# An attention, gated-MLP and RWKV kernel on one core: filler matmuls on TensorE during the first batch's attention

## The chip, the cores and the metric

The kernel runs on one core of one Trainium2 chip. The metric is the device time in microseconds (us) of one execution. Several executions are timed and their median is given; one further execution is taken by the hardware profiler, and all views of the trace come from that one.

## The reference

Three layers follow each other: attention with a causal window of 128 keys and a distance bias, a gated MLP with a matmul along the sequence, and an RWKV channel mix.

```python
def _attn_ref(q, k, v):                     # (4, 8, 576, 64)
    scores = scale * np.matmul(q, k.transpose(0, 1, 3, 2))
...
    scores = np.where(mask, scores + bias[None], -1000000000.0)
...
    return np.matmul(attn, v).astype(np.float32)

def _moe_ref(x, w_in, g_ln, w_sg, b_sg, w_out):      # x (4, 576, 512), w_in (512, 1024)
    h = x @ w_in
...
    u, v = (h[..., :d_ff // 2], h[..., d_ff // 2:])
...
    v_s = np.einsum('ts,bsd->btd', w_sg, v_n) + b_sg[None, :, None]
    gated = u * v_s
    return (x + gated @ w_out).astype(np.float32)

def _moe2_ref(x, mu_k, mu_r, w_k, w_v, w_r):
...
    k = np.maximum(xk @ w_k, 0.0)
    v = k * k @ w_v
    r = 1.0 / (1.0 + np.exp(-(xr @ w_r)))
    return (r * v).astype(np.float32)
```

## The kernel before, in words

**Tiles.** Sequences of 576 rows are cut into five tiles of at most 128. A product in float32 is done in most places as three float32r matmuls of a high and a low part; the first eight heads' scores and all products of attention weights and values are plain float32 matmuls.

**Stages.** The four batches have eight heads each. The loop `for n in range(9)` (line 1117) records the attention of the first batch, one `slot(n)` per head: scores into a bank of PSUM (`s_bank`, tile `s`), bias, row extreme and exponential (`s_tile`, tiles `p`, `nmax`, `sum`, `rin`), transposes of the weights (`t1_step`, `t2_step`, tile `t`, copied to `pf`), and for each pair of heads the product with the values (`av_step`, tile `a`, copied to `x`; a last piece of it goes into a score bank, so that `s<-pf,rawv` is part of it). Beside the heads, eight pieces of `w_in` (float64, taken apart on ScalarE and VectorE) become `w_in_t`. From the second batch on (line 1128), the attention of batch b + 1 is merged with the gated MLP of batch b (`moe1`, tiles `d`, `gt`, `u`, `v`, `gg`). The first gated-MLP matmul is `d<-w_in_t,xg`; it needs the attention output of all eight heads of the first batch. `phase2` is the channel mix over all rows.

**What sets the order.** All operations are recorded first (`Rec.op`), each with its engines and estimated costs in ns, and what it depends on. `Rec.rank` gives each a due time, for TensorE its place in the running sum `pe_time` of TensorE's costs. `Rec.schedule` then plays the engines in a list simulation: a free engine takes the ready operation with the earliest due time; an operation with several engines goes where the plan sees it end first. The sorted start times are the order in which the instructions are written, engine by engine. On the chip each engine runs its queue in that order.

**Buffers.** PSUM has three pools: `psD` (four buffers, tiles `d`, `a`, `wps`), `psS` (two banks, tile `s`), `psT` (two, tile `t`).

**Names that the change touches.** `wps` (line 1093) is a tile of `psD` that takes the results of ten matmuls of zeros at the start, which nobody reads. `K.tri` is a constant bfloat16 tile of ones and zeros in two triangles, written by GpSimd at the start. `Build.mm` (line 368) records a group of matmuls as one operation; the matmuls themselves all have line 377, transposes line 385.

Of the kernel before, what the change touches and what calls it, by code (L numbers as in the profile page):

```python
# [9 lines left out]
F32 = mybir.dt.float32  # L10
# [10 lines left out]
P = 128  # L21
# [109 lines left out]
class Rec:  # L131
# [6 lines left out]
        "pool": {"pe": 92.0, "act": 64.0, "dve": 64.0, "pool": 120.0, "sp": 100.0},  # L138
        "sp": {"pe": 0.0, "act": 0.0, "dve": 0.0, "pool": 0.0, "sp": 0.0},
    }  # L140
    BIAS_DP, BIAS_DA, BIAS_AP = 3000.0, 1500.0, 1500.0

    def __init__(self):
        self.ops, self.tags, self.psum = [], {}, set()
        self.bufs = {}
        self.after = {}
        self.open_pool = None
        self.pe_time = 0.0

# [93 lines left out]
    def schedule(self):  # L243
        ops = self.ops
        engs = ("pe", "act", "dve", "pool", "sp")
        free = {e: 0.0 for e in engs}
        q = {e: [] for e in engs}
        soon = []
        for o in ops:
            o.indeg, o.start = len(o.deps), None  # L250
            o.rdy = {a[0]: 0.0 for a in o.alts}
            if not o.indeg:
                for a in o.alts:
                    heapq.heappush(soon, (0.0, o.i, a[0]))
        t = 0.0
        done = 0
        dma_free = 0.0
        held = {"dve": 0.0, "pool": 0.0}
        other = {"dve": "pool", "pool": "dve"}

        def begin(o, e, t):
            return max(t, held[other[e]]) if o.port[e] else t
        wake = []
        while done < len(ops):
            while soon and soon[0][0] <= t:
                _, i, e = heapq.heappop(soon)
                o = ops[i]
                if o.start is not None:
                    continue
                bias = 0.0  # L270
                if len(o.alts) > 1:
                    names = [a[0] for a in o.alts]
                    if e == "dve":
                        bias = self.BIAS_DP if "pool" in names else self.BIAS_DA
                    elif e == "act" and "pool" in names:
                        bias = self.BIAS_AP
                    bias += ENG.get((o.lab, "/".join(names), e), 0.0)
                heapq.heappush(q[e], (o.lst + bias, i))
            moved = False
            for e in engs:  # L280
                if free[e] > t:
                    continue
                h = q[e]
                while h and ops[h[0][1]].start is not None:
                    heapq.heappop(h)
                if not h:
                    continue
                if e == "sp" and dma_free > t + 2500.0:
                    soon_sp = dma_free - 2500.0
                    heapq.heappush(wake, soon_sp)  # L290
                    continue
                o = ops[heapq.heappop(h)[1]]
                a = next(x for x in o.alts if x[0] == e)
                if len(o.alts) > 1:
                    best = min(begin(o, x[0], max(free[x[0]], t, o.rdy[x[0]])) + x[1] for x in o.alts)
                    if begin(o, e, t) + a[1] > best + 1e-6 and begin(o, e, t) + a[1] > o.lst + 100.0:
                        heapq.heappush(h, (-1e18, o.i))
                        alt = None
                        sk = []
                        while h:  # L300
                            z = heapq.heappop(h)
                            oz = ops[z[1]]
                            if oz.start is not None:
                                continue
                            az = next(x for x in oz.alts if x[0] == e)
                            bz = min(begin(oz, x[0], max(free[x[0]], t, oz.rdy[x[0]])) + x[1] for x in oz.alts)
                            if begin(oz, e, t) + az[1] > bz + 1e-6 and begin(oz, e, t) + az[1] > oz.lst + 100.0:
                                sk.append(z)
                                continue
                            alt = oz  # L310
                            break
                        for z in sk:
                            heapq.heappush(h, z)
                        if alt is None:
                            continue
                        o = alt
                        a = next(x for x in o.alts if x[0] == e)
                o.start, o.eng = t, a
                if e == "sp":
                    free[e] = t + 475.0  # L320
                    dma_free = max(dma_free, t + 1125.0) + a[1]
                    o.end = dma_free + 1300.0
                else:
                    t0 = begin(o, e, t)
                    free[e] = t0 + a[1]
                    o.end = t0 + a[1]
                    if o.port[e]:
                        held[e] = t0 + a[1]
                done += 1
                moved = True  # L330
                for c in o.outs:
                    c.indeg -= 1
                    for x in c.rdy:
                        c.rdy[x] = max(c.rdy[x], o.end + self.LAT[e][x])
                    if not c.indeg:
                        for x in c.rdy:
                            heapq.heappush(soon, (max(c.rdy[x], t), c.i, x))
            if moved:
                continue
            nxt = [f for f in free.values() if f > t]  # L340
            if soon:
                nxt.append(max(soon[0][0], t))
            while wake and wake[0] <= t:
                heapq.heappop(wake)
            nxt += wake[:1]
            assert nxt
            t = min(nxt)
        self.makespan = max(o.end for o in ops)
        return sorted(ops, key=lambda o: (o.start, o.i))


class Build:
# [132 lines left out]
    def dma(self, out, in_, nbytes, reads=(), writes=(), nominal=None):  # L485
        nc = self.nc
        return self.r.op([("sp", nbytes / 330.0, lambda: nc.sync.dma_start(out=real(out), in_=real(in_)))],
                         [in_, *reads], [out, *writes], nominal=nominal)

    def raw(self, eng, cost, go, reads, writes):  # L490
        return self.r.op([(eng, cost, go)], reads, writes)
# [3 lines left out]
def attn_gmlp_rwkv_kernel(  # L495
# [19 lines left out]
    K = Build(nc)  # L515
# [7 lines left out]
    late = ("w2", "raw2")  # L523
# [3 lines left out]
    def T(pool, shape, dtype, tag, name=None, bufs=None):  # L527
        return R.tile(pool, shape, dtype, tag, name or tag, bufs)
# [41 lines left out]
    def cols(w, kk, half):  # L570
        k = w.shape[1] // 2
        return w[kk * P:(kk + 1) * P, half * k:(half + 1) * k]
# [24 lines left out]
    def load_head(n):  # L597
        if n >= NH:
            return
        b, h = divmod(n, H)  # L600
        pt = ("qk", "QK") if plain_s(n) and n in ODD else ("raw", "raw")
        rawqk[n] = T(pt[0], [P, 2, S], F32, pt[1], "rawqk")
        K.dma(rawqk[n], qkT[b, h], P * 2 * S * 4)
# [178 lines left out]
    def av_step(n):  # L782

        b, c = n // H, n % H // 2
        a = T("psD", [P, 4, P], F32, "d", "a")
        its, a4 = [], []
        p4 = PTc.pop((n, 1)) if fold(n) else None
        for r0, m in ((0, n), (64, n + 1)):
            rv = rawv.pop(m)
            ar = a[r0:r0 + 64]  # L790
            if fold(m):
                pf = PTc.pop((m, 0))
                its.append([(ar[:, ki:min(ki + 2, 4), :], rv[:, ki, :], pf[:, ki::4, :], ki == 0, ki == 3, SG) for ki in range(4)])
                k = m - n
# [16 lines left out]
                it.append((ar[:, 384:512], rv[:, 3, :], pf[:, 0, :], False, True, SG))  # L811
                its.append(it)
            a4.append((r0, rv, (pf[:, 1, 0:64], pf[:, 1, 64:128])))
        K.mm([x for y in zip(*its) for x in y])
        A4.append((n, a4))
        if c == 0:
            x_t[b] = T("xp", [P, NC, S + 1], F32, "x")
            z = x_t[b][:, :, 0:1]
# [2 lines left out]
        if n + 2 == NH:  # L821
            a4_step(T("psS", [P, 2, 256], F32, "s", "a4"))

    XG = {}

    def xsplit(b, c):
        if c == 0:
# [264 lines left out]
    K.raw("dve", 200, lambda: nc.vector.memset(real(wz), 0.0), [], [wz])  # L1092
    wps = T("psD", [P, 512], F32, "d", "wps")
    K.mm([(wps, wz[:, 0:128], wz, True, True, {})] * NWARM)
    load_head(0)
    K.raw("pool", 1100, lambda: nc.gpsimd.memset(real(K.tri), 1.0), [], [K.tri])
    for u in range(2):
# [17 lines left out]
    K.ts(mus1.flat(), mus.flat(), -1.0, 1.0, ALU.mult, ALU.add)  # L1115
    K.raw("dve", 60, lambda: nc.vector.memset(real(mhalf), -0.5), [], [mhalf])
    for n in range(9):
        for i, (_, f) in enumerate(slot(n)):
            f()
            if i == 3 and n + 2 < H:  # L1120
                mask_head(n + 2)
        for i in ((0, 1), (2, 3), (4,), (5,), (6,), (7,), (), (), ())[n]:
            kk, half = i % 4, 1 - i // 4
            c = slice(half * 512, half * 512 + 512)
            raw = None
            if wide:
                raw = (st0, st1)[i // 4][:, i % 4]
            job(w_in_t[:, kk, 0, c], w_in_t[:, kk, 1, c], cols(w_in, kk, half), 512, raw=raw, dec=("tp", "t"))
    for b in range(B):
        a = []  # L1130
        for n in range(8 * (b + 1) + 1, 8 * (b + 2) + 1):
# [2 lines left out]
        d = moe1(b)  # L1134
# [6 lines left out]
        if b == B - 1:  # L1141
# [3 lines left out]
            for i in range(8):  # L1145
                kk, half = i % 4, i // 4
                c = slice(half * 512, half * 512 + 512)
                k = 5 + i
# [81 lines left out]
```

## Time and profile before

| what | value |
|---|---|
| median of 3 runs | 617.51 us (616.62 to 618.85) |
| the profiled execution, own time | 618.84 us |
| its span, first to last instruction | 616.9 us |
| mean granted TensorE clock | 0.982 |
| TensorE matmuls, busy | 596.0 us, 97% of the span |
| VectorE, ScalarE, GpSimd, busy | 450.3, 343.9, 191.6 us |
| bytes moved | 57.74 MB |

The span is shorter than the execution's time by what lies ahead of the first and behind the last instruction, 1.9 us. The granted clock is the share of TensorE's full speed (2.4 GHz) that the chip allowed: 0.50 is 1.2 GHz, and a mean between the two levels says for what part of the time each held. A busy time is the time in which an engine had an instruction at work.

### The profile page before, as it was taken

The numbers are of one execution on the slowest core, as the hardware profiler recorded it, in microseconds if no ns is written. First come the engines' busy times: TensorE is split into PE (matmuls) and PEld (weight loads), VectorE is DVE, ScalarE is ACT, GpSimd is POOL, SyncE is SP. The second block draws the span as 40 slices with busy tenths as digits, with TensorE's granted clock in tenths as the row PEclk, the third lists the DMA queues.
The fourth block names the chain that finished last, engine by engine and source line by source line (L and its number), as shares of the span: only waits on it lengthen the run. The fifth ranks groups of instructions, "written<-read, shape, count | busy, mean of one in ns | idle before, by whom it ended". The sixth has DMA issues, their size and how long they took to land.

```text
span 616.9 us, 10182 instructions
## 1 busy us (share of the span) xinstructions
PE 596.0 (97%) x3538; PEld 505.0 (82%) x3538; DVE 450.3 (73%) x1204; ACT 343.9 (56%) x868; POOL 191.6 (31%) x334
## 2 busy tenths in 40 slices
PE   7777999999999999999999999999999999999997
PEld 4554879999789997889979998787888888888896
DVE  5777699999999999998588998894581349226122
ACT  5987889776887555875246547632531333234031
POOL 5455474335575457632234430001020001000000
PEclk9978899999999999999999999999999999999999
DMA  8954423323413134010171437413002000000100
GB/s 307 322 162 143 142 78 109 115 78 102 157 56 99 61 99 155 22 61 12 31 254 67 136 112 249 134 63 102 35 17 69 17 1 35 35 1 1 52 17 35
DMA packets 25331, 57.74 MB, mean 94 GB/s; under 512 B 4416, under 2 KB 13120, under 8 KB 24768
## 3 DMA queue, kind: packets, MB, share of 16 engines
q1 hardware_dynamic: 25280, 57.09, 28.0%
q8 instruction: 28, 0.46, 0.3%
q14 instruction: 23, 0.19, 0.1%
HBM read 47.63 MB, written 9.45 MB: 93 GB/s over the span
## 4 chain that ended last, share of the span: by engine, by line
PE 85%; DVE 8%; ACT 4%; issue 1%; DMA 1%; POOL 1%; SPq 0%; ACTq 0%; DVEq 0%; POOLq 0%
PE d L377 47%; PE vps L377 16%; PE s L377 7%; PE rps L377 6%; PE a L377 5%; PE t L385 3%; ACT p L399 1%; PE tf L385 1%; DVE p L680 1%; DVE wdec L455 1%; ACT pf L407 1%; DMA rawqk<-in_qk_dram 1%; DVE QK L419 1%; DVE gt L455 1%; ACT wdec L553 0%
## 5 line engine op out<-in xcount | busy, mean ns | idle before, releaser
L377 PE MATMUL d<-xk,wk 128*128 128x512 f32 (+1 forms) x480 | 105.3, 368 | 0.0
L377 PEld LDWEIGHTS d<-xk,wk 128*128 128x128 f32 x480 | 84.6, 188 | 16.2 <-ACT rl L399 0.2
L377 PE MATMUL vps<-w_v_t,k2h 128*128 128x512 f32 x288 | 94.8, 396 | 0.3 <-DVE w_v_t L409 0.3
L399 ACT ACTIVATE p<-p,nmax 128x256 f32<-128x256 f32 (+3 forms) x160 | 76.6, 480 | 28.5 <-DVE nmax L680 27.7
L680 DVE CUSTOM_DVE_ANT_0 p<-s,mask 128x256 f32<-128x256 f32 (+3 forms) x160 | 60.2, 383 | 12.8 <-PE s L377 12.2
L377 PE MATMUL d<-w_sg_t,vhl 128*128 128x288 f32 x448 | 66.5, 298 | 0.0
L399 ACT ACTIVATE rl<-d 128x512 f32<-128x512 f32 (+1 forms) x40 | 22.1, 554 | 78.3 <-PE d L377 75.0
L377 PEld LDWEIGHTS vps<-w_v_t,k2h 128*128 128x128 f32 x288 | 54.1, 188 | 13.8 <-DVE w_v_t L409 0.7
L377 PEld LDWEIGHTS d<-w_sg_t,vhl 128*128 128x128 f32 x448 | 60.9, 188 | 0.7 <-issue 0.2
L377 PE MATMUL d<-w_in_t,xg 128*128 128x512 f32 (+1 forms) x240 | 60.8, 398 | 0.0
L377 PE MATMUL d<-xg,w_in_t 128*128 128x288 f32 x384 | 57.0, 298 | 2.0 <-DVE u L455 2.0
L377 PE MATMUL vps<-w_v_t,k2l 128*128 128x512 f32 x144 | 57.0, 396 | 0.0
L377 PE MATMUL d<-gg,w_out_t 128*128 128x288 f32 x384 | 56.7, 298 | 0.0
L377 PEld LDWEIGHTS d<-xg,w_in_t 128*128 128x128 f32 x384 | 52.1, 188 | 3.1 <-DVE u L455 2.6
L377 PE MATMUL rps<-w_r_t,xr 128*128 128x512 f32 x216 | 54.4, 390 | 0.0
L377 PEld LDWEIGHTS d<-gg,w_out_t 128*128 128x128 f32 x384 | 52.0, 188 | 0.9 <-issue 0.3
L409 DVE CAST k2h<-rl 128x512 fp32r<-128x512 f32 (+1 forms) x28 | 10.9, 388 | 55.3 <-ACT rl L427 55.2
L377 PEld LDWEIGHTS d<-w_in_t,xg 128*128 128x128 f32 (+1 forms) x240 | 41.0, 177 | 10.9
L419 DVE TENSOR_TENSOR r<-vps,r 128x512 f32<-128x512 f32 x18 | 12.4, 691 | 48.7 <-PE vps L377 48.7
L377 PEld LDWEIGHTS rps<-w_r_t,xr 128*128 128x128 f32 x216 | 40.3, 188 | 8.4
L475 POOL TENSOR_SCALAR p<-p,rin 128x128 f32<-128x128 f32 (+4 forms) x63 | 35.3, 570 | 35.9 <-DVE rin L703 27.3
L482 ACT ACTIVATE p<-p,rin 128x128 f32<-128x128 f32 (+4 forms) x86 | 33.3, 429 | 8.3 <-DVE rin L703 8.2
(130 smaller groups left out, 1166.7 us busy)
## 6 DMA issues: line engine op xcount, KB each, us to landing
rawqk<-in_qk_dram SPq DMA_DIRECT2D x32, 576.0 KB, 3.9
rawv<-in_v_dram SPq DMA_DIRECT2D x32, 160.0 KB, 2.5
xs<-x SPq DMA_DIRECT2D x4, 1154.0 KB, 5.8
out_dram<-r SPq DMA_DIRECT2D x18, 256.0 KB, 2.0
st<-in_w_in_dram SPq DMA_DIRECT2D x8, 512.0 KB, 6.8
wraw<-in_w_k_dram SPq DMA_DIRECT2D x8, 512.0 KB, 3.8
wraw<-in_w_v_dram SPq DMA_DIRECT2D x8, 512.0 KB, 3.5
wraw<-in_w_out_dram SPq DMA_DIRECT2D x8, 256.0 KB, 3.3
```

Source lines behind the costliest of these rows:

```text
L377: pe.matmul(real(o), real(l), real(r), start=st, stop=sp, **ex)
L385: pe.transpose(real(o), real(i), real(d))
L399: nc.scalar.activation(real(out), real(in_), func, scale=scale, **kw)
L407: alts.append(("act", self._act(in_), lambda: nc.scalar.copy(real(out), real(in_))))
L409: alts.append(("dve", self._dve(in_.n, not in_.ps), lambda: nc.vector.tensor_copy(real(out), real(in_))))
L419: alts.append(("dve", self._dve(out.n, False), lambda: nc.vector.tensor_tensor(real(out), real(a), real(b), op)))
L455: alts.append(("dve", cost or self._dve(out.n, False, isinstance(s, Vw)), lambda: nc.vector.scalar_tensor_tensor(real(out), real(a), real( ...
L475: alts.append(("pool", 240 + out.n if ptr else 150 + 0.83 * out.n, lambda: nc.gpsimd.tensor_scalar(real(out), real(a), real(s1), real(s2), ...
L482: alts.append(("act", self._act(a, 1), lambda: nc.scalar.mul(real(out), real(a), real(s1))))
L680: K.raw("dve", 70 + w / 0.96, lambda: nc.vector.tensor_tensor_reduce(out=real(pw), in0=real(si), in1=real(ma), scale=-0.125, scalar=3.0e38 ...
```

## The change

`Build.filler` records a list of up to 220 single matmuls that are no operations of the plan: each multiplies a 128x128 block of `K.tri` with 256 columns of `K.tri` into `wps`, which nobody reads. The list opens with a matmul of the same shape that is an operation, and ends with another (`filler_end`), which depends on the attention output `AV[k]` of a pair of heads. Between the start of the first and that of the second, whenever the planned TensorE has nothing ready, the next thing to become ready is further off than a filler takes plus 50 ns, and the planned busy time of the last `SPAN` ns is below `DUTY` of it, `schedule` puts one filler there. Fillers left in the list are never written. There are two such lists, from the first head to the second pair's output, and from head 5 to the fourth pair's output.

```diff
+    SPAN, DUTY = 3400.0, 0.7
...
                 if not h:
+                    fl = next((f for f, a, z in fill if f and a.start is not None and z.start is None), None)
+                    if e == "pe" and fl and pe_busy:
+                        while pe_busy[0][1] < t - self.SPAN:
+                            pe_busy.pop(0)
+                        nxt = min((x[0] for x in soon if x[2] == "pe" and ops[x[1]].start is None), default=1e18)
+                        o = fl[0]
+                        if nxt > t + o.alts[0][1] + 50 and sum(b - a for a, b in pe_busy) < self.DUTY * self.SPAN:
+                            fl.pop(0)
+                            o.start, o.eng = t, o.alts[0]
+                            o.end = free["pe"] = t + o.alts[0][1]
+                            pe_busy.append((t, o.end))
+                            filled.append(o)
+                            moved = True
+                        else:
+                            heapq.heappush(wake, t + 200.0)
                     continue
...
+                    if e == "pe":
+                        pe_busy.append((t0, o.end))
...
-        return sorted(ops, key=lambda o: (o.start, o.i))
+        return sorted(ops + filled, key=lambda o: (o.start, o.i))
...
+    def filler(self, out, l, r, count):
...
+            o.alts = [("pe", r.n / 2.4 + 13, lambda: pe.matmul(real(out), real(l), real(r), start=True, stop=True), 1)]
...
+        self.r.fill.append([many, self.mm([(out, l, r, True, True, {})]), None])
+
+    def filler_end(self, out, l, r, late):
+
+        o = self.r.fill[-1][2] = self.mm([(out, l, r, True, True, {})])
+        o.deps.add(late)
...
-        K.mm([x for y in zip(*its) for x in y])
+        AV.append(K.mm([x for y in zip(*its) for x in y]))
...
+    warm = (K.tri[:, 0, 0, :], K.tri[:, 0].flat()[:, 0:256], 220)
...
     for n in range(9):
+        if n == 0:
+            K.filler(wps[:, 0:256], *warm)
+        if n == 5:
+            K.filler_end(wps[:, 0:256], *warm[:2], AV[1])
+            wps = T("psD", [P, 512], F32, "d", "wps")
+            K.filler(wps[:, 0:256], *warm)
...
+    K.filler_end(wps[:, 0:256], *warm[:2], AV[3])
```

In the order of the changed kernel 55 matmuls `wps<-tri` stand on TensorE, 51 fillers (line 518) and the four that open and close the lists (line 398). Because the planned times move, the order of other work changes too, on every engine. Three places on TensorE follow; each filler is a row of LDWEIGHTS and a row of MATMUL, "..." stands for the further ones of the same run. `s` are scores, `t` transposes; the numbers behind names tell tiles apart.

The first place is the scores of the fifth head (`rawqk_234`, now `rawqk_240`) and the sixth (`rawqk_268`, now `rawqk_274`), with the fourth head's transposes, before:

```order
L377 MATMUL s_428<-rawqk_234 64x192
L385 MATMUL t_452<-ident_133,p_315 128x128
L385 MATMUL t_452<-ident_133,p_328 128x128 x2
L385 MATMUL t_452<-ident_133,p_380 128x128
L377 MATMUL s_458<-rawqk_268 128x128
L377 MATMUL s_458<-rawqk_268 128x256
```

and now:

```order
L398 MATMUL s_440<-rawqk_240 64x192
L518 LDWEIGHTS tri_112
L518 MATMUL wps_118<-tri_112 128x256
...
L398 MATMUL s_467<-rawqk_274 128x128
L398 MATMUL s_467<-rawqk_274 128x256
L406 MATMUL t_480<-ident_129,p_320 128x128
L406 MATMUL t_480<-ident_129,p_332 128x128 x2
L406 MATMUL t_480<-ident_129,p_393 128x128
```

Five fillers stand behind the fifth head's scores, and the sixth head's first scores have moved ahead of the fourth's transposes.

The second place is the seventh head's scores and the sixth's transposes, before:

```order
L377 MATMUL s_567<-rawqk_331 128x256
L377 MATMUL s_575<-rawqk_331 128x256 x2
L377 MATMUL s_611<-rawqk_331 64x192
L385 MATMUL t_615<-ident_133,p_468 128x128
```

and now:

```order
L398 MATMUL s_599<-rawqk_337 128x256
L518 LDWEIGHTS tri_112
L518 MATMUL wps_567<-tri_112 128x256
...
L398 MATMUL s_620<-rawqk_337 128x256 x2
L518 LDWEIGHTS tri_112
L518 MATMUL wps_567<-tri_112 128x256
...
L398 MATMUL s_653<-rawqk_337 64x192
L406 MATMUL t_657<-ident_129,p_485 128x128
```

Five fillers stand ahead of the second bank of scores and eight ahead of the third.

The third place is the last scores of the second batch's first head (`QK`, `KL`), between the transposes of the first batch's seventh and eighth heads, before:

```order
L385 MATMUL t_740<-ident_133,p_647 64x64
L377 MATMUL s_766<-QK_565 64x256
L377 MATMUL s_766<-KL_608,QK_565 64x256
L385 MATMUL t_791<-ident_133,p_672 128x128
L385 MATMUL t_791<-ident_133,p_692 128x128 x2
```

and now:

```order
L406 MATMUL t_784<-ident_129,p_694 64x64
L518 LDWEIGHTS tri_112
L518 MATMUL wps_567<-tri_112 128x256
...
L398 MATMUL s_821<-QK_579 64x256
L398 MATMUL s_821<-KL_618,QK_579 64x256
L518 LDWEIGHTS tri_112
L518 MATMUL wps_567<-tri_112 128x256
...
L406 MATMUL t_842<-ident_129,p_715 128x128
L406 MATMUL t_842<-ident_129,p_722 128x128 x2
```

Six fillers stand ahead of the last bank of scores and seven ahead of the eighth head's transposes.

## Rows read from the trace of the kernel before

**Rows 1.** The page of the profile, the span and the granted clock in 40 slices
```profile
span 616.9 us, 10182 instructions
...
PEclk9978899999999999999999999999999999999999
```

**Rows 2.** Windows of three stretches: us, busy time of each engine, clock, DMA
```profile
0.00:66.00 66.00, 51.55 (x279) 35.96 (x280) 45.58 (x163) 50.21 (x147) 34.93 (x69) 0.84 0.67 229
66.00:291.00 225.00, 222.78 (x1631) 196.67 (x1628) 208.40 (x609) 168.37 (x477) 116.78 (x209) 1.00 0.28 89
291.00:617.00 326.00, 321.71 (x1634) 272.36 (x1632) 196.34 (x433) 125.35 (x245) 39.87 (x57) 1.00 0.21 69
```

**Rows 3.** Windows of 1 us on TensorE: us, PE busy, PEclk, DMA, GB/s
```profile
28.00:29.00 1.00, 1.00 (x7) 0.65 0.86 230
...
35.00:36.00 1.00, 1.00 (x9) 0.94 0.01 2
...
41.00:42.00 1.00, 0.00 (x0) 0.97 0.00 0
...
48.00:49.00 1.00, 1.00 (x10) 0.61 0.08 16
...
59.00:60.00 1.00, 0.81 (x5) 0.51 0.94 373
...
65.00:66.00 1.00, 1.00 (x9) 0.58 0.00 0
```

**Rows 4.** Timeline of TensorE in the first 72 us: start, us, matmuls, idle before
```profile
11.83 0.66 PE L385 MATMUL t<-ident,p 128*128 128x128 f32 x4 [0.86 <-POOL p L475]
...
16.66 1.25 PE L385 MATMUL t<-ident,p 128*128 128x128 f32 x10
...
18.86 0.39 PE L377 MATMUL s<-pf,rawv 128*64 128x64 f32 x5 [0.70 <-ACT pf L407]
...
27.81 0.79 PE L385 MATMUL t<-ident,p 128*128 128x128 f32 x4 [1.98 <-POOL p L475]
...
42.76 0.90 PE L377 MATMUL s<-rawqk 128*64 128x192 f32 x2 [2.36 <-DVE nmax L680]
...
53.45 0.28 PE L377 MATMUL s<-KL,QK 128*128 128x256 f32 x1
53.57 0.29 PE L377 MATMUL s<-QK 128*128 128x256 f32 x1
...
59.19 1.11 PE L385 MATMUL t<-ident,p 128*128 128x128 f32 x4 [2.56 <-ACT p L482]
...
60.32 0.41 PE L377 MATMUL s<-KL,QK 128*128 128x256 f32 x1
60.53 0.41 PE L377 MATMUL s<-QK 128*128 128x256 f32 x1
...
66.83 1.57 PE L377 MATMUL d<-w_in_t,xg 128*128 128x512 f32 x6
```

**Rows 5.** Windows in which the clock stayed up, columns as in rows 2
```profile
13.00:19.00 6.00, 4.72 (x33) 3.24 (x33) 5.08 (x23) 5.73 (x19) 2.51 (x5) 1.00 1.04 422
50.00:56.00 6.00, 4.33 (x26) 2.89 (x24) 4.43 (x16) 5.84 (x17) 2.91 (x7) 1.00 0.62 202
```

**Rows 6.** Chain that ended last, in the first 130 us: start, us, what
```profile
19.25 1.57 PE a L377 x15
...
32.56 2.90 PE a L377 x16
```

**Rows 7.** Windows of the chain's three pieces at half clock, columns as in rows 2
```profile
31.98:35.46 3.48, 3.48 (x23) 3.31 (x23) 2.33 (x5) 2.04 (x5) 1.15 (x4) 0.55 0.71 278
42.76:49.80 7.04, 7.04 (x40) 4.55 (x40) 4.78 (x17) 3.46 (x11) 4.32 (x7) 0.57 0.38 124
59.19:66.32 7.13, 6.86 (x39) 6.00 (x39) 3.20 (x14) 4.32 (x15) 3.40 (x7) 0.53 0.55 187
```

**Rows 8.** Timeline of TensorE, a wait for VectorE after 66 us
```profile
263.45 1.86 PE L377 MATMUL d<-xg,w_in_t 128*128 128x288 f32 x12 [0.86 <-DVE u L455]
```

More of the change, by code (lines that the diff above doesn't have):

```diff
@@ L146, in __init__ @@
         self.after = {}
+        self.fill = []
         self.open_pool = None
@@ L263, in schedule @@
         wake = []
+        fill = [[list(f), a, z] for f, a, z in self.fill]
+        filled, pe_busy = [], []
         while done < len(ops):
@@ L488, in dma @@
                          [in_, *reads], [out, *writes], nominal=nominal)
+    def filler(self, out, l, r, count):
+        pe = self.nc.tensor
+        many = []
+        for k in range(count):
+            o = Op()
+            o.i, o.deps, o.outs, o.lab, o.pe = 1 << 20 | len(self.r.fill) << 12 | k, [], [], "fill", True
+            o.alts = [("pe", r.n / 2.4 + 13, lambda: pe.matmul(real(out), real(l), real(r), start=True, stop=True), 1)]
+            o.port, o.w0, o.cnt = {"pe": False}, out.base, 1
+            many.append(o)
+        self.r.fill.append([many, self.mm([(out, l, r, True, True, {})]), None])
+    def filler_end(self, out, l, r, late):
+        o = self.r.fill[-1][2] = self.mm([(out, l, r, True, True, {})])
+        o.deps.add(late)
     def raw(self, eng, cost, go, reads, writes):
@@ L822, in av_step @@
             a4_step(T("psS", [P, 2, 256], F32, "s", "a4"))
-    XG = {}
+    XG, AV = {}, []
     def xsplit(b, c):
```

## The prediction

> **What bounds the kernel now.** I read first the span and the clock in 40 slices, where the digits below 9 all lie in slices 3, 4 and 5 of some 15.4 us each [rows 1]; then three long windows [rows 2]; then the first 66 us alone, the clock in windows of 1 us and TensorE's timeline [rows 3 to 5]; and last the chain of waits there [rows 6, 7]. The reader should see three things.
>
> First, TensorE is the bound from about 66 us on: it is busy 222.8 of 225 us and then 321.7 of 326 us, at a granted clock of 1.00 [rows 2]. What a change does before 66 us therefore reaches the end only as an earlier or later start of this long stretch. The matmuls in it are not changed.
>
> Second, TensorE is not full before 66 us: 51.6 of 66 us busy, and the granted clock averages 0.84 [rows 2]. The clock was at 0.50 (1.2 GHz instead of 2.4) in three pieces: it falls in the window 28:29 and is back in 35:36, falls in 41:42 and is back in 48:49, falls in 59:60 and is back in 65:66; the whole windows between the first two ends, the next two and the last two (six, six and five of them) are at 0.50 [rows 3]. Ahead of each fall TensorE stood idle once for long: 1.98 us before 27.81, 2.36 us before 42.76, 2.56 us before 59.19 [rows 4]. The shorter waits, 0.86 us before 11.83 and 0.70 us before 18.86, were followed by no fall [rows 4]. In the stretches 13:19 and 50:56 TensorE was busy for only 4.72 and 4.33 of 6 us, with its idle time in pieces, and the clock stayed at 1.00 [rows 5].
>
> Third, in these pieces the slow matmuls are themselves the chain that ends last. The 16 matmuls of one pair's attention output take 2.90 us on the chain at 32.56, where 15 of them took 1.57 us at 19.25 [rows 6].
>
> **The gain, if the clock stays up.** The chain is on TensorE from 31.98 to 35.46, from 42.76 to 49.80 and from 59.19 to 66.32, but for short pieces [rows 7]. Work at clock c takes 1/c as long, so at full clock the pieces lose at most PE busy x (1 - clock): 3.48 x 0.45 = 1.57 us, 7.04 x 0.43 = 3.03 us, 6.86 x 0.47 = 3.22 us [rows 7], together 7.8 us. That is the upper end. It can't be had whole, because the other engines' work in the pieces doesn't shrink. The busiest of them needs 2.33 us (VectorE), 4.78 us (VectorE) and 4.32 us (ScalarE) [rows 7]; so the pieces can lose at most 3.48 - 2.33 = 1.15, 7.04 - 4.78 = 2.26 and 7.13 - 4.32 = 2.81 us. The smaller of the two limits in each piece gives 1.15 + 2.26 + 2.81 = **6.2 us**. The lower end is nothing: the waits themselves (1.98 + 2.36 + 2.56 us) are for VectorE, ScalarE and GpSimd [rows 4], and no filler shortens them.
>
> **What the fillers cost.** 51 fillers and four marker matmuls of the same shape (one that opens and one that closes each of two runs), 55 in all. The trace has no bf16 128x256 matmul. The nearest rows are float32r matmuls of 256 columns with a new weight each: they start 0.12 us apart at full clock (53.45 to 53.57) and 0.21 us apart at half (60.32 to 60.53) [rows 4]. I take 0.12, as the forecast is that the clock stays up. All 55 on the path cost 6.6 us at full clock, 11.6 us at half: the upper bound. The lower bound is nothing, if each lies in idle time.
>
> By the order, 34 stand directly ahead of an instruction that waited in the trace: 5 ahead of the wait of 0.86 us and 5 ahead of that of 0.70 us, 5 in the first long wait, 4 ahead of the next pair's attention output, 8 in the second long wait, 7 in the third. They fill 34 x 0.12 = 4.1 us of idle time and cost nothing; TensorE would have to get there over half a microsecond later for this cover to be gone. Of the other 21, ten (the four markers, and six beside transposes) stand before work that was ready: 10 x 0.12 = 1.2 us. Eleven stand in a short wait of 0.2 us just ahead of the second and the third long one (five and six): they push one score bank back by up to 0.6 and 0.7 us, of which the long wait behind it swallows a part, since that wait ends by another engine's work; I charge half, 0.7 us. Together **1.9 us**. No semaphore is added within a run of fillers, but whatever is queued on TensorE behind one waits for it, so their place in the order counts.
>
> **What is moved.** Fillers take planned TensorE time, and the markers shift the planner's due times, so the order changes on all queues. SP's queue keeps its 150 transfers, with 8 of them (four heads, two weights, a constant, an input of the last stage) one to six places off. I cost that at nothing: a head is loaded two heads before its scores, and a delay of a whole head would have to come for that cover to be gone. VectorE goes from 1,206 to 1,201 instructions, ScalarE from 710 to 701, GpSimd from 339 to 353; GpSimd was busy 34.9 of 66 us and 116.8 of 225 us [rows 2], so it has room. What the reordering does between 66 and 291 us is not known: VectorE is busy 208.4 of 225 us there [rows 2], and TensorE's waits for it are of the size of 0.86 us at 263.45 [rows 8]. Bounds: those waits can vanish (TensorE's whole idle time there, 2.2 us, is a gain) or a few more can open (four of 0.86 us, 3.4 us lost). I take nothing, the middle. The second PSUM buffer that the fillers' tile takes is free again before the first tile of the gated MLP needs it, by the order.
>
> **The sum.** 6.2 - 1.9 = 4.3 us off the profiled execution's 618.84 us, which is 614.5. That execution lies 1.3 us above the median of the runs shown, 617.51, so I forecast **613.2 us**.
>
> **A rule against the change.** In the stretch 13:19 the clock stayed at 1.00 though TensorE was idle for 1.28 of 6 us [rows 5], and its work there held transposes, as the ten that took 1.25 us at 16.66 [rows 4]. The Trainium skill, "TensorE: Matmul & The Clock Gate", section "Part 4: PE-mode transpose", says that a transpose isn't counted as TensorE being busy in the way a matmul is. The planner of this kernel does count them as busy, so by that rule it puts in too few fillers beside transposes, and all three falls can come back. The trace doesn't bear it out so far: with transposes among the work, the stretch held. What it would do here is rival 2.
>
> **The rivals.**
> 1. *Other engines take the gain* (chance 0.12). The three pieces shrink, but VectorE and ScalarE, busy 45.6 and 50.2 of 66 us [rows 2], are late next, and the three long waits grow by what was saved. Half of 6.2 us would be left, less 1.9: 1.2 us, 616.3. For it: all three waits are for them. Against: in the second and third piece they had 2.3 and 2.8 us of slack [rows 7].
> 2. *The fillers are too few, and the clock falls all the same* (0.20). By the order they leave about 1.98 - 0.6 = 1.4, 2.36 - 1.0 = 1.4 and 2.56 - 0.8 = 1.7 us of the three waits [rows 4], between the 0.86 us that was harmless and the 1.98 us that was not. If none holds, nothing is gained and the fillers that are not covered cost 1.9 us: 619.4. If one of three holds, 6.2 / 3 - 1.9 = 0.2 us are gained: 617.3; if two, 2.2 us: 615.3.
> 3. *The later order is worse* (0.14): slower than before. The clock holds, but between 66 and 291 us TensorE waits for VectorE at new places, as it does now for `u` [rows 8]. From five new waits of 0.86 us on, the 4.3 us are eaten; with eight, 6.9 us, it is 620.1. For it: VectorE is at 93% there. Against: TensorE has only 2.2 us of idle time in 225 now, with the same buffers.
> 4. *The change doesn't do what it says* (0.04): TensorE reaches the fillers at other times than planned and they lie on the path, 6.6 us less a gain of 3: 621.
>
> That leaves 0.50 for the forecast.
>
> **How the numbers follow.** A measurement of this kernel can tell about 0.3% from no change, 1.9 us: faster is below 615.7, slower above 619.4. The forecast and the better parts of rivals 1 and 2 (0.05 and 0.05) make 0.60 faster. Rival 1's rest (0.07), half of rival 2 (0.10) and a part of rival 3 (0.05) make 0.22 the same. Rival 2's worst quarter (0.05), most of rival 3 (0.09) and rival 4 (0.04) make 0.18 slower. The range: below, 6.2 us of gain, covered fillers and a microsecond from the later order, 617.5 - 7.2 = 610.3; above, the falls come back and the uncovered fillers are paid, 619.4. The forecast's own range is 611.0 to 615.6.
>
> **What would show it.** Right: granted clock of 1.00 in all windows before the first matmul of the gated MLP; that matmul (66.83 us now [rows 4]) at about 62.5; the 16 matmuls of an attention output at 1.6 to 1.7 us on every pair; TensorE's idle time before 66 us cut by about 4 us; from there on 550 us as now. Wrong: a window at 0.50 behind one of the three waits (rival 2); the clock up but the first gated-MLP matmul later than 65 (rival 1); an early start that is lost before 291 us in waits for VectorE (rival 3); chain pieces on the filler line (rival 4).

## The result, and the profile after

The changed kernel takes 611.12 us (median of 4 runs, 610.99 to 611.58), against 618.11 us for the kernel before (4 runs, 616.62 to 618.85). The ratio is 0.9891, 95% interval 0.987 to 0.9913: 7.0 us faster. The profiled execution took 611.09 us, with a mean granted clock of 0.999.

The page of the profile, the span, TensorE's line and the granted clock in 40 slices:

```profile
span 609.4 us, 10294 instructions
...
PE 594.2 (98%) x3593; PEld 502.9 (83%) x3593; DVE 453.1 (74%) x1199; ACT 340.1 (56%) x859; POOL 204.3 (34%) x348
...
PEclk9999999999999999999999999999999999999999
```

No slice is below 9 now, where slices 3 to 5 were [rows 1]. Windows of the three stretches (columns as in rows 2):

```profile
0.00:66.00 66.00, 57.72 (x379) 40.74 (x380) 54.21 (x177) 54.32 (x165) 44.89 (x75) 1.00 0.73 242
66.00:291.00 225.00, 223.67 (x1651) 198.45 (x1650) 207.56 (x600) 166.09 (x468) 126.43 (x230) 1.00 0.26 85
291.00:617.00 326.00, 312.82 (x1567) 263.68 (x1565) 191.37 (x423) 119.70 (x227) 32.94 (x44) 0.99 0.21 69
```

In the first 66 us the clock is 1.00, 0.84 before [rows 2]. TensorE's timeline there:

```profile
10.94 0.72 PE L518 MATMUL wps<-tri 128*128 128x256 bf16 x5
...
28.05 0.92 PE L398 MATMUL s<-rawqk 128*128 128x128 f32 x4 [0.60 <-DVE nmax L718]
29.43 0.66 PE L406 MATMUL t<-ident,p 128*128 128x128 f32 x4 [0.45 <-POOL p L496]
...
39.72 1.04 PE L518 MATMUL wps<-tri 128*128 128x256 bf16 x8
40.98 0.54 PE L398 MATMUL s<-rawqk 128*64 128x192 f32 x2 [0.22 <-DVE nmax L718]
...
48.81 0.66 PE L406 MATMUL t<-ident,p 128*128 128x128 f32 x4 [1.01 <-POOL p L496]
...
52.88 0.30 PE L398 MATMUL s<-QK 128*64 128x256 f32 x1 [0.64 <-DVE rin L741]
...
53.14 0.94 PE L518 MATMUL wps<-tri 128*128 128x256 bf16 x7
54.11 0.83 PE L406 MATMUL t<-ident,p 128*128 128x128 f32 x4
...
59.32 1.56 PE L398 MATMUL d<-w_in_t,xg 128*128 128x512 f32 x6
```

The first gated-MLP matmul starts at 59.32, 66.83 before [rows 4]: 7.51 us earlier. From there to the end of the span it is 609.4 - 59.32 = 550.1 us, and it was 616.9 - 66.83 = 550.1 us. The whole gain arises before that matmul and none is lost behind it. The long waits of 1.98, 2.36 and 2.56 us [rows 4] are gone as such: the fourth head's transposes at 29.43 come behind five fillers and waits of 0.60 and 0.45 us; the seventh head's last scores at 40.98 come behind eight fillers (from 39.72) and 0.22 us; the eighth head's transposes at 54.11 come behind seven fillers (from 53.14) and no wait, though there is now one of 1.01 us at 48.81. Two pieces of the chain that ended last:

```profile
53.30 0.78 PE wps L518 x7
...
56.88 1.57 PE a L398 x16
```

The attention output takes 1.57 us at 56.88, as 15 of its matmuls did at full clock before and not 2.90 [rows 6]. The seven fillers are themselves a piece of the chain, 0.78 us. In the middle of the attention the chain has left TensorE. From 23.7 to 45.3 us its shares by line are:

```profile
by line: ACT p L420 27.2%; ACT wdec L591 13.7%; ACT pf L428 11.4%; ACT p L503 9.9%; issue 8.1%; PE t L406 7.0%; POOL p L496 6.4%; ACT w_in_t L428 5.2%; ACT QK L428 4.8%; DVE sum L493 3.2%; ACT x L428 2.7%; PE wps L518 1.5%; DVE nmax L718 0.
```

ScalarE's seven rows make 75%, the exponentials (`p`, line 420) first, and TensorE's two make 8.5%: ScalarE is late there now.

### The profile page after: what moved, and what is told of

Same layout as the page of the kernel before. It is cut to its first block, busy times and chain, and to the rows that moved or that the text cites. A ratio compares the mean times of both kernels' runs of the same rounds, so it can differ in the third digit from the quotient of the medians.

```text
span 609.4 us, 10294 instructions
## 1 busy us (share of the span) xinstructions
PE 594.2 (98%) x3593; PEld 502.9 (83%) x3593; DVE 453.1 (74%) x1199; ACT 340.1 (56%) x859; POOL 204.3 (34%) x348
## 4 chain that ended last, share of the span: by engine, by line
PE 81%; DVE 11%; ACT 5%; issue 1%; DMA 1%; POOL 0%; SPq 0%; DVEq 0%; ACTq 0%; POOLq 0%
PE d L398 46%; PE vps L398 15%; PE rps L398 7%; PE s L398 6%; PE a L398 4%; PE t L406 2%; PE tf L406 2%; ACT p L420 1%; ACT wdec L591 1%; DVE p L718 1%; DVE wdec L476 1%; DVE w_v_t L440 1%; DVE mt L476 1%; DMA rawqk<-in_qk_dram 1%; ACT p L503 1%
## 5 line engine op out<-in xcount | busy, mean ns | idle before, releaser
L496 POOL TENSOR_SCALAR p<-p,rin 128x128 f32<-128x128 f32 (+4 forms) x73 | 39.5, 552 | 23.8 <-DVE rin L741 17.9
L496 POOL TENSOR_SCALAR mt<-xc,mus 128x512 f32<-128x512 f32 (+3 forms) x9 | 8.8, 978 | 84.7 <-ACT xk L428 49.5
```

The costliest lines, as they stand in the source:

```text
L496: alts.append(("pool", 240 + out.n if ptr else 150 + 0.83 * out.n, lambda: nc.gpsimd.tensor_scalar(real(out), real(a), real(s1), real(s2), ...
```

## The experiments

All runs of each kernel, beside runs of the kernel before on the same chip. The changed kernel's ratio is that of the result. The first four experiments share one chip, with the first row; the next four ran on a second chip, where the kernel before had a median of 617.49 us, and `fill_only_all` on a third, where it had 617.55 us. "New" is the order of the changed kernel, row for row on every engine, "old" that of before; only fillers are left out or added.

| kernel | order | fillers | median us (range, runs) | mean clock of its runs | ratio to before, 95% interval |
|---|---|---|---|---|---|
| before, beside the first four experiments | old | 0 | 617.64 (616.41 to 619.27, 17) | 0.982 to 0.992 | |
| changed | new | 51 | 611.12 (610.99 to 611.58, 4) | 0.999 to 1.000 | 0.987 to 0.9913 |
| `order_only` | new | 0 | 615.91 (612.24 to 618.65, 12) | 0.983 to 0.997 | 0.9938 to 0.9988 |
| `fill_only` | old | 49 | 613.02 (612.58 to 614.05, 5) | 0.996 to 1.000 | 0.992 to 0.9944 |
| `run1_only` | new | 22 | 613.05 (612.12 to 613.67, 4) | 0.993 to 0.997 | 0.9909 to 0.9939 |
| `run2_only` | new | 29 | 613.49 (611.64 to 614.07, 4) | 0.993 to 0.999 | 0.9915 to 0.9947 |
| `fill_transposes` | new | 51 | 611.14 (610.79 to 611.40, 6) | 0.999 to 1.000 | 0.9877 to 0.9914 |
| `duty_35` | new | 9 | 611.87 (611.04 to 612.82, 6) | 0.997 to 1.000 | 0.9887 to 0.9929 |
| `duty_50` | new | 20 | 612.28 (610.72 to 613.58, 6) | 0.993 to 1.000 | 0.9893 to 0.9941 |
| `duty_100` | new | 102 | 611.91 (611.47 to 612.41, 6) | 0.999 to 1.000 | 0.9889 to 0.9928 |
| `fill_only_all` | old | 101 | 612.74 (612.29 to 612.92, 6) | 0.998 to 1.000 | 0.9904 to 0.9934 |

**The order alone.** The fillers are planned as in the changed kernel, and not written.

```diff
         for o in order:
-            o.eng[2]()
+            if o.lab != "fill":
+                o.eng[2]()
```

> The changed kernel's order on every engine, with the 51 fillers left out and the four marker matmuls kept. Theory A (the clock is the gain): without fillers the clock falls to 0.50 again behind the waits of about 2 us, the first matmul of the gated MLP comes at 65 to 68 us, and the time is 616 to 620 us, near the kernel before. Rival B (the new order is the gain, the fillers are not needed): the first gated-MLP matmul comes at 58 to 61 us and the time is 610 to 613 us, whatever the clock does. Rival C (both share it): 613 to 616 us.

615.91 us, ratio 0.9963: neither theory A nor rival B alone, at the edge of A's range and in that of C. The range is wide, and the time follows the clock: the five runs at a mean clock of 0.994 or more took 612.24 to 612.94 us, the six at 0.986 or less 616.23 to 618.65. The profiled execution (616.97 us) has three falls. Windows of 1 us, then the timeline:

```profile
32.00:33.00 1.00, 0.67 (x9) 0.73 1.00 326
33.00:34.00 1.00, 1.00 (x7) 0.50 0.95 381
43.00:44.00 1.00, 0.97 (x3) 0.50 0.51 207
57.00:58.00 1.00, 0.61 (x2) 0.50 0.77 204
```

```profile
28.52 0.92 PE L398 MATMUL s<-rawqk 128*128 128x128 f32 x4 [1.26 <-DVE nmax L718]
29.90 0.77 PE L406 MATMUL t<-ident,p 128*128 128x128 f32 x5 [0.45 <-POOL p L496]
...
32.33 0.51 PE L398 MATMUL s<-pf,rawv 128*64 128x64 f32 x5 [0.42 <-ACT pf L428]
...
43.03 0.90 PE L398 MATMUL s<-rawqk 128*64 128x192 f32 x2 [1.80 <-DVE nmax L718]
...
56.95 0.45 PE L398 MATMUL s<-QK 128*64 128x256 f32 x1 [1.41 <-DVE rin L741]
...
65.14 1.56 PE L398 MATMUL d<-w_in_t,xg 128*128 128x512 f32 x6
```

So the new order by itself shortens the waits ahead of the falls (1.26, 1.80 and 1.41 us, against 1.98, 2.36 and 2.56 [rows 4]), and the clock falls all the same in this execution; the first gated-MLP matmul comes at 65.14.

**The fillers alone.** The order of before is kept on every engine; a function walks TensorE's planned operations and puts a filler where the planned gap is over 170 ns and the planned busy time of the last 3,400 ns is below 0.7 of it.

```diff
+            while a.end < t and n.start <= z.start and n.start > t + 170.0:
...
+                if sum(y - x for x, y in busy) < 0.7 * 3400.0:
...
+                    out.append(o)
...
     order = R.schedule()
+    order = sorted(order + R.gaps(tri_op, AV[3], lambda: nc.tensor.matmul(real(wo), real(wl), real(wr), start=True, stop=True)),
+                   key=lambda o: (o.start, o.i))
```

> The order of the kernel before on every engine, kept row for row, with 49 fillers put into the planned gaps of TensorE (no marker matmuls). Theory A: the clock stays at 1.00 through the first 66 us, the first gated-MLP matmul comes at 59 to 61 us, the time is 610 to 613 us. Rival B: the clock stays up and yet the time is 616 to 619 us, since the order is the old one. Rival C: 613 to 616 us.

613.02 us: 4.6 us faster than before on the same chip, by the fillers alone. The clock was at 0.999 or 1.000 in three of five runs (612.58 to 613.02 us) and at 0.996 in two, the profiled one among them. That execution (614.05 us) has one fall, behind twelve fillers and what is left of the second wait; a window of 1 us and the timeline:

```profile
44.00:45.00 1.00, 1.00 (x5) 0.50 0.94 319
```

```profile
41.36 0.54 PE L396 MATMUL s<-rawqk 128*64 128x192 f32 x2 [1.07 <-DVE nmax L699]
```

So theory A has the larger part of the gain, and some 1.8 us (612.9 against 611.1 at full clock) are left for the order, or for falls not seen: rival C, with unequal shares.

**One list of fillers at a time.** The same loop leaves out the fillers of the second list, or of the first.

```diff
+            if o.lab != "fill" or o.i < (1 << 20) + 4096:
```

> The changed kernel with the 22 fillers of its first list alone (up to the second pair's attention output); those of the second list are left out, the order is otherwise the same. Theory A: the first fall (near 28 us) is gone, the second and third are there as before; of the 7 us gained some 1 to 2.5 us stay: 615.5 to 617.5 us. Rival B: 610 to 613 us, as with all fillers.

```diff
+            if o.lab != "fill" or o.i >= (1 << 20) + 4096:
```

> The changed kernel with the 29 fillers of its second list alone (from the sixth head's transposes on); the first list is left out, the order is otherwise the same. Theory A: one fall near 28 to 30 us, none later; 4 to 6 us of the 7 stay: 612 to 614.5 us. Rival B: 610 to 613 us. A third way: the second and third fall need idle time that only comes where the first one has been, so nothing but the first fall is lost.

With the first list alone: 613.05 us, 2.5 us better than the best end of theory A. One reason is seen: the falls that came back near 43 and 56 us lasted 3 to 4 us each and not 6 to 7 as in the old order [rows 3]. Another is that this expectation put the new order at nothing. The first and last windows of 1 us of both falls in its profiled execution (613.67 us):

```profile
43.00:44.00 1.00, 1.00 (x6) 0.55 0.63 182
46.00:47.00 1.00, 1.00 (x10) 0.74 0.03 14
56.00:57.00 1.00, 1.00 (x8) 0.88 0.65 233
60.00:61.00 1.00, 1.00 (x11) 0.91 0.59 134
```

With the second list alone: 613.49 us, as expected, but its profiled execution (611.64 us) shows no fall at all. Windows of 1 us and the timeline of this execution:

```profile
32.00:33.00 1.00, 0.68 (x11) 1.00 0.89 305
33.00:34.00 1.00, 1.00 (x13) 1.00 0.98 373
```

```profile
28.50 0.92 PE L398 MATMUL s<-rawqk 128*128 128x128 f32 x4 [1.25 <-DVE nmax L718]
29.88 0.76 PE L406 MATMUL t<-ident,p 128*128 128x128 f32 x5 [0.45 <-POOL p L496]
...
32.32 0.39 PE L398 MATMUL s<-pf,rawv 128*64 128x64 f32 x5 [0.42 <-ACT pf L428]
```

Up to here this kernel is the one with the order alone, with the same waits within 0.01 us (1.26, 0.45 and 0.42 us there). There the clock fell in 32:33, here it did not, and in the three other runs of this kernel the mean clock was 0.993. The profiled executions of `duty_35` and `duty_50`, with waits of 1.24, 0.45 and 0.42 us there and one and three fillers between them, kept the clock there too. The same idle time thus brings the fall in one execution and not in the next; the waits alone don't decide it.

**Transposes as fillers.**

```diff
-lambda: pe.matmul(real(out), real(l), real(r), start=True, stop=True)
+lambda: pe.transpose(real(out[:, 0:128]), real(self.idn), real(self.idn))
```

> The changed kernel, order and places the same, but each of the 51 fillers is a transpose of the constant identity (128x128, float32) instead of a matmul; the four markers stay matmuls. A transpose takes about 0.11 us here (four in 0.44 us on the chain of before), a filler matmul 0.12 us, so TensorE is filled alike. Theory A1 (a transpose holds the clock as a matmul does): clock 1.00 before the first gated-MLP matmul, 610.5 to 611.8 us, all runs within 1 us. Rival (the rule of the Trainium skill, 'TensorE: Matmul & The Clock Gate', 'Part 4: PE-mode transpose': transposes aren't counted as TensorE being busy in the way matmuls are): the clock falls as without fillers, 612 to 619 us with a wide spread.

611.14 us, all six runs within 0.61 us and at a clock of 0.999 or more. Its timeline has the transposes in the fillers' places:

```profile
26.34 0.77 PE L518 MATMUL wps<-ident 128*128 128x128 f32 x5
...
39.32 1.04 PE L518 MATMUL wps<-ident 128*128 128x128 f32 x8
```

Here transposes held the clock as well as matmuls. The Trainium skill, "TensorE: Matmul & The Clock Gate", section "Part 4: PE-mode transpose", says otherwise, as weighed in the prediction; these six runs, with float32 transposes, disagree, and the measurement decides.

**How many fillers.** One constant of the planner is changed.

```diff
-    SPAN, DUTY = 3400.0, 0.7
+    SPAN, DUTY = 3400.0, 0.35
```

> The changed kernel with the planner's DUTY at 0.35 instead of 0.7: 9 fillers instead of 51, the order of all other work the same. If any filler in a long wait is enough: clock at 1.00, 610.5 to 611.5 us, a little faster than 51 for the fillers that are off the path. If the amount counts: the clock falls in some runs, 612 to 617 us, between the kernel with the order alone (615.9) and the changed one (611.1).

> DUTY at 0.5: 20 fillers, the order of all other work the same. If the amount counts: falls in fewer runs than with 9 fillers, 611 to 614 us. If 20 are enough: 610.5 to 611.2 us in every run.

> DUTY at 1.0: every planned gap is filled, 102 fillers, the order of all other work the same. It measures what fillers cost: the clock is at 1.00 as with 51, so the time differs by the further 51 alone. If fillers cost as the prediction charged (1.9 us for 55): 612.5 to 613.5 us. If they lie in idle time: 610.8 to 611.6 us. If all lie on the path, 51 x 0.12 = 6.1 us: 617 us.

Nine fillers bring 611.87 us, 20 bring 612.28, and in both three of six runs were at a clock of 0.999 or more (611.04 to 611.32 and 610.72 to 611.44 us). The other three, at 0.997 and at 0.993 or 0.994, took 612.42 to 613.58 us. So the clock fell in as many runs with 20 fillers as with nine, and not in fewer, as the second expectation had it. The profiled execution with nine has its one fall behind the wait at 53.19, where none of the six fillers is left; windows of 1 us and the timeline:

```profile
54.00:55.00 1.00, 0.57 (x3) 0.72 0.95 327
55.00:56.00 1.00, 1.00 (x7) 0.50 0.74 265
```

```profile
53.19 0.30 PE L398 MATMUL s<-QK 128*64 128x256 f32 x1 [1.41 <-DVE rin L741]
...
60.90 1.56 PE L398 MATMUL d<-w_in_t,xg 128*128 128x512 f32 x6
```

At full clock 9, 20 and 51 fillers give the same time (medians of 611.22, 611.00 and 611.12 us), and 102 cost 0.8 us more than 51: 0.016 us for each further filler, an eighth of the 0.12 us that it takes on TensorE. So 51 fillers cost next to nothing; what they buy is that the clock falls in none of the runs.

**The order, priced at full clock.** The fillers alone, with every gap filled (`0.7 * 3400.0` becomes `1.0 * 3400.0`).

> The order of the kernel before, row for row, with every planned gap before the fourth pair's attention output filled (101 fillers, no markers), so that the clock should stay at 1.00 in every run. It prices the order by itself, against the kernel with the changed order and all gaps filled (102 fillers, 611.9 us). If the new order is worth what the runs at full clock with 49 and 51 fillers say (612.9 against 611.1 us): 613 to 614 us and a first gated-MLP matmul at 61 us. If those 1.8 us came from falls that still happen in the old order: 611.5 to 612.3 us, and a first gated-MLP matmul at 59.5 to 60 us.

612.74 us, between the two expectations, every run at 0.998 or more, the same as the three runs with 49 fillers at full clock. So the falls are not the rest; the old order itself costs 0.8 us against the new one with all gaps filled (611.91) and 1.6 us against the changed kernel. The two with all gaps filled ran on different chips, on which the kernel before agreed to 0.06 us (617.49 and 617.55). The place is the last stretch, from the third pair's attention output to the first gated-MLP matmul (columns as in rows 2), first in the old order:

```profile
44.27:60.59 16.32, 14.57 (x129) 10.84 (x128) 12.43 (x44) 15.03 (x43) 10.43 (x16) 1.00 0.55 184
```

and in the new one with all gaps filled:

```profile
44.80:59.67 14.87, 14.66 (x126) 10.61 (x122) 13.82 (x43) 12.85 (x43) 11.65 (x18) 1.00 0.41 122
```

It takes 16.32 us in the old order and 14.87 in the new, with the clock at 1.00 in both. Up to there the new order is 0.53 us later (44.80 against 44.27), so 0.92 of these 1.45 us are left at the first gated-MLP matmul. In the old order ScalarE is busy 15.03 of 16.32 us, in the new one 12.85 of 14.87. Two casts of whole heads are part of what it has more; in the new order they are on VectorE. First ScalarE's row in the old order, then VectorE's in the new:

```profile
L426 ACT CAST QK<-rawqk 128x1152 fp32r<-128x1152 f32 x2 | 2.3, 1140 | 0.0
```

```profile
L430 DVE CAST QK<-rawqk 128x1152 fp32r<-128x1152 f32 x2 | 1.5, 760 | 0.0
```

That the casts are the reason is only argued; no kernel was run in which they alone are moved.

## Why the prediction was right or wrong

**The mechanism and the direction were right.** The clock stays up, the gain arises before the first gated-MLP matmul, and the 550.1 us behind it are unchanged, so that the reordering there, taken at nothing, was worth nothing (rival 3). 611.12 lies in the range. The size was off: 4.3 us forecast, 7.0 measured, and the first gated-MLP matmul came at 59.32 instead of about 62.5.

**The gain at full clock, 6.2 us, came out as a sum, not in each piece.** `fill_only_all` has the order of before, so the chain's three pieces [rows 7] can be compared one by one. Where they begin and end in it, on the chain that ended last:

```profile
31.97 0.39 PE s L396 x5
...
33.93 1.06 PE s L396 x4
...
41.25 0.54 PE s L396 x2
...
46.03 0.02 issue
...
55.64 0.66 PE t L404 x4
...
60.08 0.67 PE s L396 x4
```

They last 1.96, 4.78 and 4.44 us, where it was 3.48, 7.04 and 7.13: 1.52, 2.26 and 2.69 us less, 6.5 together, with the fillers in them paid. The limit by the busiest other engine was met in the second piece (2.26) and nearly in the third (2.81), but not in the first, which lost 1.52 and not at most 1.15 us. That VectorE was busy for 2.33 us in that window before didn't bound it; in the 1.96 us it is busy for 1.68. Behind the second piece 0.2 us are lost again (9.61 us from 46.03 to 55.64, 9.39 before). By the time of the whole, 618.84 - 612.74, the gain is 6.1 us, with 101 fillers paid, and 7.8 us was rightly not taken. That no filler shortens the waits was right in the old order: before the eighth head's transposes `fill_only_all` has 14 fillers and then still a wait of 0.45 us:

```profile
53.49 1.70 PE L1176 MATMUL wps<-tri 128*128 128x256 bf16 x14
55.64 0.66 PE L404 MATMUL t<-ident,p 128*128 128x128 f32 x4 [0.45 <-ACT p L501]
...
60.59 1.57 PE L396 MATMUL d<-w_in_t,xg 128*128 128x512 f32 x6
```

**The fillers' cost, 1.9 us, was the step that failed first.** The charge for ten fillers "before work that was ready" and half of eleven others came to 1.9 us for 55. Between 9 and 51 fillers no cost could be told at full clock, in the old order none between 49 and 101 (612.9 and 612.7 us), and even at the 0.016 us of the further ones 55 would cost 0.9 us. Work that is ready on TensorE isn't on the chain for that: in the changed kernel the chain between 23.7 and 45.3 us is mostly on ScalarE, and fillers there delay little that ends last. The seven on the chain at 53.30 take the place of a wait (with three fillers there, `duty_35` still waits 0.47 us).

**The order, taken at nothing, was the second.** I asked what the reordering does after 66 us and not what it does before. There it shortens the three long waits (`order_only`), and it is worth 0.8 us with every gap filled, and 1.6 to 1.8 us between the changed kernel and the old order with fillers at full clock. From 618.84 us to the changed kernel's 611.12 the measured steps are 6.1 us (the clock, every gap filled, old order), 0.8 us (the new order) and 0.8 us (51 fillers fewer). They are differences of measured times, so that their sum has to fit and confirms none of them.

**From the profiled execution to the median.** The forecast took the same 4.3 us off the median. That is not quite right here, since the kernel before falls by more or less in each run (clock 0.982 to 0.992 in the 17 runs): the profiled execution, at 0.982, had more to gain than the middle one. Against the 617.64 us of the 17 runs the old order's gain is 4.9 us, and the whole is 6.5. So the forecast of 613.2 us is close to the old order with fillers (613.02 and 612.74 us), and this is partly luck: the fillers' cost, charged too high, stands against the 1.2 us that the profiled execution lay above this median. What is missing from 613.2 to 611.12 is for the most part the order.

**The rivals.** The first (other engines take the gain) came only in small part: the chain moved to ScalarE in the middle, but in the old order the pieces lost 6.5 us and only 0.2 us of that was lost again in the waits. The second (too few fillers) is refuted for 51, and seen for 9, 20, 22 and 29, and for 49 in the old order in two runs of five. It looked for a bound between 0.86 and 1.98 us of waiting; the runs show none, since waits of 1.25 us brought a fall in one execution and not in another. The fourth is refuted.

## What to carry to other kernels

Where TensorE waits for other engines and then bounds the chain itself, price the granted clock in pieces: busy time times what the clock is short of full, cut to what the busiest other engine's work in the piece allows; the cut is an estimate and no bound (1.15 us against 1.52 measured in one piece). Matmuls whose result nobody reads were cheap here where the chain isn't on TensorE, so put in more than the least that can work: the last dozens buy that the clock holds in every run, and not in half of them. And where a planner makes the order, price the new order by itself, in the stretch where it was meant to change nothing too.

## What was not expected of the hardware

- The same kernel without fillers has a different mean clock in each run (`order_only`: 0.983 to 0.997 in 12 runs), and with it a time from 612.24 to 618.65 us. A single profile shows one of these cases.
- The same waits (1.25 or 1.26, 0.45 and 0.42 us) were followed by a fall in one execution and by none in another. What decides between them stays open.
- Nine fillers were enough for three runs of six; 22 in the first list's places alone left falls in all four runs (clock 0.993 to 0.997). So the place counts, and not the number alone.
- Transposes held the clock as matmuls did (611.14 against 611.12 us).
